# First chunk in halves of 64 times too, from one table of powers; the own key as a product of its own

## The chip, the cores and the metric

The kernel runs on one core of a Trainium2 chip. A core has a matrix engine (PE, whose weight loads are listed as PEld), a vector engine (DVE), a scalar engine (ACT), a general engine (POOL) and a queue engine (SP) that issues the transfers here. They run side by side; each works through its own list of instructions in order, and semaphores make one wait for another. [...] The metric is the device time of one execution in microseconds (us); lower is better.

## The reference, cut to what matters

An RWKV-style recurrence is followed by an MLP with gelu, all in fp32. Batch 4, 8 heads, 768 times, head size 48; the MLP has 384 inputs, 2048 hidden units and 384 outputs.

```python
for t in range(S):
    kt, vt, rt = (k[:, :, t], v[:, :, t], r[:, :, t])
    cur = np.einsum('bhd,bhe->bhde', u[None] * kt, vt)
    y[:, :, t] = np.einsum('bhd,bhde->bhe', rt, state + cur)
    state = w[None, :, :, None] * state + np.einsum('bhd,bhe->bhde', kt, vt)
...
x = y with the heads side by side            # 3072 tokens x 384
h = x @ w_in
g = 0.5 * h * (1.0 + erf(h / sqrt(2)))
return g @ w_out
```

`w` is a decay per head and channel. A key at time s counts at a later time t with the weight w^(t-1-s); the own key, at time t itself, counts with `u` in its place.

## The kernel before, in words

**Tiling.** Time is cut into six chunks of C = 128. A group is one pair of heads in one chunk, with all four batches, so there are 24 groups: `gi // 4` is the chunk, `PAIRS[gi % 4]` the pair. The 512 outputs (4 batches x 128 times) of the four groups of a chunk make one token tile of the MLP. The MLP of a tile is 16 steps over the hidden units, 96 steps in all. Each fp32 operand is split in a high and a low part (`wh`/`wl`, `xx`, `gh`/`gl`), and a step has 18 matmuls of 128x512: nine for the first layer into the bank `Hp` (`product1`, L602, three operand combinations times three parts of x) and nine for the second layer into the banks `O[0]` to `O[2]` (`product2`, L642). ACT reads `Hp` twice (L630 gives `gh`, L631 gives `gf`), and DVE makes `gl` of the two (L632). In the order of the program, PE does the nine first-layer matmuls of step m, then the nine second-layer matmuls of step m-1, in three operations of three, while ACT does the two gelu passes of step m. After 16 steps ACT and DVE copy the three `O` banks out (L676).

**The weights.** `w_split` takes each of the 16 weight pieces through passes on ACT (L330, L332, L340) and DVE (L334, L336, L338, L342), all within the first token tile.

**A group of chunks 1 to 5** (`prepare`, `products`, `state`, `past_scores`, `finish`) works in halves of 64 times. DVE multiplies r and k by powers of w from a table `E` (L479). POOL makes the key times its state power (L485) and the product r*k*u (L482, L488), DVE sums that over the channels (L491), and ACT spreads the sums on the diagonal of `Am` (L351). PE makes the scores of r with the scaled keys of the same half (L527), and DVE selects those of the past into `Am` (L576). PE adds up the output from the state before each half (L519, `old`) and from `Am` and v (L546, `new`), and makes the gain of the state in each half (L536, `gains`). DVE carries the state over a half (L569). `keep` splits the output into its high part on ACT (L367) and its low part on DVE (L368). The outputs lie in the PSUM tile `YU`, scores and gains in `AA`.

**A group of chunk 0** (`first_group`) works on all 128 times at once, with a table `W` of powers from -64 to 64: inverses by reciprocal (L271), scaling of r and k on DVE and POOL (L393), r*k (L399) and its sum with u on PE (L404), the diagonal on ACT, DVE or POOL (L351, L356), scores (L419), selects (L425), outputs (L439), state gains (L445). State powers are made on DVE (L281 to L285), turned by PE (L290) and copied (L293). The table `E` for the later chunks is cut out of `W` by eight transfers on SP's queue (L303).

**What sets the order.** `Plan` is a list scheduler written into the kernel: each step names its engine, a cost, a due time, and what it reads and writes by name (`"H"`, `"O0"`, `"Y"`). `Plan.run` emits the steps in the order of its own clock, with a lag (`LAG`) between engines, and fills gaps of PE with matmuls on zeros into `Hp` (L249, `heat`). The waits themselves are not made from these names. The Tile framework makes them from the tiles that each instruction reads and writes, in the order in which the steps are emitted.

**PSUM tiles before.** Two tiles have two banks each, and four have one:

```python
AA = psp.tile([128, 2, 512], F32, name="A")
YU = psp.tile([128, 2, 512], F32, name="Y")
Y, U = (YU[:, i] for i in range(2))
Hp = psp.tile([128, 512], F32, name="Hp")
O = [psp.tile([128, 512], F32, name=f"O{i}") for i in range(3)]
```

In chunk 0 the bank `Y` holds outputs, and `U` holds turned powers and state gains; the profile names both by their tile, "Y".

Of the kernel before, what the change touches and what calls it, by code (L numbers as in the profile page):

```python
# [27 lines left out]
HALF = 64  # L28
LP = 112
# [4 lines left out]
NEAR = 4  # L34
KEYS = C + 2
# [4 lines left out]
LOADS = (1, 2, 3, "w0", "w1", "u", 4, 5, "w2")  # L40

SCALE = ("pd", "d", "dd", "p")
PRODUCT = ("p", "p", "d", "p")
BONUS = ("pa", "aa", "pd", "pa")


class Plan:
# [6 lines left out]
    def __init__(self):  # L54
        self.ops, self.writer, self.readers, self.reads, self.filler = [], {}, {}, [], None
# [28 lines left out]
    def run(self):  # L84
# [14 lines left out]
        for _ in self.ops:  # L99
# [9 lines left out]
            if e == "pe" and self.filler:  # L109
                fill, buf, ns, room = self.filler  # L110
                while not unread and max(free[e], clear) + room < start:
                    fill()
                    free[e] = max(free[e], clear) + ns
# [9 lines left out]
            if self.filler:  # L123
                unread += sum(self.filler[1] in self.reads[m] for m in users[n])
# [10 lines left out]
def rwkv_gelu_mlp(tc, rkT, rkv, wuT, uN, wmlp, r, k, vT, w, u, out):  # L135
    nc = tc.nc
    with ExitStack() as ctx:
# [17 lines left out]
        wu_sb = sb([LP, 3 * NP], F32, "wu_sb", cst)  # L155
        w_sb = wu_sb[:, 0:NP]
        u_pair = wu_sb[:, NP:].rearrange("l (p j) -> l p j", j=2)
# [8 lines left out]
        W = sb([LP, NP, KEYS + C], F32, "W", pro)  # L166
        WKs = W[:, :, KEYS:]
        E = sb([LP, 2, NP, 2, HALF], F32, "E")
        P128 = sb([LP, NP], F32, "P128")
        WN = sb([C, NP, 2, D], F32, "WN", pro)  # L170
        WN2 = sb([C, NP, 2, D], F32, "WN2")
        T = [sb([LP, 2, NB, C], F32, f"T{i}", pro) for i in range(NP)] + [sb([LP, 2, NB, C], F32, f"Tb{i}") for i in range(2)]
        Ts = [sb([LP, 2, NB, C], F32, f"Ts{i}", pro) for i in range(NP)]
        RK = [sb([LP, NB, C], F32, f"RK{i}", pro) for i in range(NP)]
        N = [sb([C, 2, NB, 2 * D], F32, f"N{i}", pro) for i in range(NP)] + [sb([C, 3, NB, 2 * D], F32, f"Nb{i}") for i in range(2)]
        Am = [sb([C, 2, NB, C], F32, f"Am{i}") for i in range(2)] + [sb([C, 2, NB, C], F32, f"Am{i}", pro) for i in (2, 3)]
        cs = [sb([C, NB * 2], F32, f"cs{i}") for i in range(4)]
# [28 lines left out]
        def load_group(gi, at):  # L206
            s = slot(gi)
            dma(LP * 4096, at, lambda: nc.sync.dma_start(T[s], rkT[gi]), w=[f"T{s}"])
            if gi < NP:
                dma(C * 3072, at + 1, lambda: nc.sync.dma_start(N[s], rkv[gi, :, 1:]), w=[f"Nk{s}", f"Nv{s}"])  # L210
            else:
# [9 lines left out]
        def select(dst, base, cm, op):  # L221
# [14 lines left out]
        add("dve", 300, -20, lambda: nc.vector.memset(zeros.bitcast(F32), 0.0), w=["zeros"])  # L236
# [14 lines left out]
        def warm_up():  # L251
            for n in range(HEATS):
                heat((A + O + [Y, U])[n % 7])
            plan.filler = lambda: heat(Hp), "H", HEAT_NS, HEAT_ROOM

        add("pe", 430 * HEATS, 10, warm_up, r=["zeros"], w=["H", "A0", "A1", "O0", "O1", "O2", "Y", "U"])


        def powers():
            nc.vector.memset(W[:, :, HALF:HALF + 1], 1.0)  # L260
            nc.vector.tensor_scalar(out=W[:, :, HALF + 1:HALF + 2], in0=w_sb.unsqueeze(2), scalar1=WMIN, scalar2=WMAX,
                                    op0=ALU.max, op1=ALU.min)
            n = 1
            while n < HALF:
                pn = W[:, :, HALF + n:HALF + n + 1].to_broadcast([LP, NP, n])
                nc.vector.tensor_tensor(out=W[:, :, HALF + n + 1:HALF + 2 * n + 1],
                                        in0=W[:, :, HALF + 1:HALF + n + 1], in1=pn, op=ALU.mult)
                n *= 2

        def inverse(p0, p1):  # L270
            nc.vector.reciprocal(out=W[:, p0:p1, 0:HALF], in_=W[:, p0:p1, C:HALF:-1])  # L271

        add("dve", 1500, 5, powers, r=["w_sb"], w=["P"])
        first = PAIRS[0]
        add("dve", 480, 6, lambda: inverse(first, first + 1), r=["P"], w=[f"W{first}"])
        for p in PAIRS[1:]:
            add("dve", 480, LATER, lambda p=p: inverse(p, p + 1), r=["P"], w=[f"W{p}"])


        def state_powers():  # L280
            nc.vector.tensor_copy(out=WKs[:, :, 0:32], in_=W[:, :, 96:C])  # L281
            nc.vector.tensor_tensor(out=P128.unsqueeze(2), in0=W[:, :, C:C + 1], in1=W[:, :, C:C + 1], op=ALU.mult)
            nc.vector.tensor_tensor(out=WKs[:, :, 32:96], in0=W[:, :, HALF:C],
                                    in1=W[:, :, C:C + 1].to_broadcast([LP, NP, HALF]), op=ALU.mult)
            nc.vector.tensor_tensor(out=WKs[:, :, 96:C], in0=W[:, :, HALF:96],  # L285
# [609 lines left out]
```

## Time and profile before

| what | value |
|---|---|
| three timed runs | 513.5, 515.7 and 517.62 us; median 515.7 |
| the profiled execution | 512.43 us, of which the span from first to last instruction is 510.7 |
| busy PE, DVE, ACT, POOL | 488.2, 248.8, 213.6 and 88.6 us |
| mean granted clock of PE | 0.973 of full speed |
| first matmul of the MLP | 37.59 us after the span's start |
| gelu of the last step of the first token tile | at 126.94 us |

How to read the lines of the profile: a timeline row gives start, length, engine, line of the kernel, operation, output<-inputs by the names of the tiles, shapes and a count; where an engine had been idle, the end of the row names in brackets how long, and whose work released it. Consecutive matmuls of one line are put together in one row; their ends are modelled, so that rows of a running PE overlap, and the distance between the starts of rows is the pace. A window row gives, for a stretch, the busy time of each engine with its instructions, then the granted clock, the share of the transfers and their rate.

### The profile page before, as it was taken

The page shows a single profiled execution, that of the slowest core. Times are in us where ns is not written, and L with a number is a line of the kernel's source. Part 1 is how long each engine was busy: PE and PEld are TensorE (multiplying, and loading weights), DVE is VectorE, ACT ScalarE, POOL GpSimd, SP SyncE. Part 2 cuts the span into 40 slices and gives each one's busy share as a digit, 9 for nine tenths or more (in the row PEclk, how much of TensorE's full clock was granted, in tenths as well). Part 3 has the DMA queues.
Part 4 walks back from the last instruction along what each step waited for, and adds up shares of the span by engine and source line. Part 5 has one row for each costly group of instructions (what it writes and reads, how often), then busy time and mean ns, then how long its engine had stood idle before and what let it go on. Part 6 is the DMA issues. An engine that isn't in the chain of part 4 may idle for free.

```text
span 510.7 us, 10489 instructions
## 1 busy us (share of the span) xinstructions
PE 488.2 (96%) x4524; PEld 387.8 (76%) x4524; DVE 248.8 (49%) x363; ACT 213.6 (42%) x472; POOL 88.6 (17%) x80
## 2 busy tenths in 40 slices
PE   5998898999999999999999999999999999999995
PEld 4876676766778778787777778778778787888884
DVE  8959999998536424614425435424424311211111
ACT  2458758774444243333343443343442322322221
POOL 5850311213022022202022022022022000000000
PEclk8659999999999999999999999999999999999998
DMA  8864574822402303403302403303403000100001
GB/s 226 254 251 145 189 231 149 252 83 63 145 7 89 94 4 92 145 1 94 95 1 94 142 5 94 94 1 94 134 13 94 13 0 12 62 1 0 1 0 67
DMA packets 15107, 45.04 MB, mean 88 GB/s; under 512 B 3728, under 2 KB 4112, under 8 KB 15056
## 3 DMA queue, kind: packets, MB, share of 16 engines
q1 hardware_dynamic: 15056, 44.32, 27.8%
q8 instruction: 37, 0.61, 0.5%
q14 instruction: 14, 0.11, 0.1%
HBM read 37.16 MB, written 4.72 MB: 82 GB/s over the span
## 4 chain that ended last, share of the span: by engine, by line
PE 84%; DVE 11%; issue 2%; ACT 1%; DMA 1%; SPq 0%; DVEq 0%
PE Hp L602 37%; PE O L642 35%; PE Y L546 2%; PE Y L519 2%; PE A L527 2%; DVE wa L338 1%; DVE wl L342 1%; DVE Ts L393 1%; PE A L536 1%; PE Y L642 1%; DVE gl L632 1%; DVE wa L336 1%; DMA T<-in_rkT_dram 1%; DVE wa L334 1%; ACT wh L340 1%
## 5 line engine op out<-in xcount | busy, mean ns | idle before, releaser
L602 PE MATMUL Hp<-xx,wh 128*128 128x512 f32 x576 | 168.8, 400 | 0.8 <-ACT gf L631 0.5
L632 DVE TENSOR_TENSOR gl<-gf,gh 128x512 fp32r<-128x512 f32 x95 | 73.2, 770 | 193.9 <-ACT gf L631 193.8
L630 ACT ACTIVATE gh<-Hp 128x512 fp32r<-128x512 f32 x95 | 56.7, 597 | 183.6 <-PE Hp L602 183.5
L602 PEld LDWEIGHTS Hp<-xx,wh 128*128 128x128 f32 x576 | 105.8, 188 | 26.6 <-ACT gf L631 1.5
L642 PE MATMUL O<-gh,wh 128*128 128x512 f32 (+1 forms) x285 | 82.0, 395 | 6.2 <-ACT gh L630 6.2
L602 PE MATMUL Hp<-xx,wl 128*128 128x512 f32 x288 | 84.1, 399 | 0.7 <-DVE wl L342 0.3
L642 PE MATMUL O<-gh,wl 128*128 128x512 f32 (+1 forms) x285 | 80.8, 391 | 0.0
L642 PE MATMUL O<-gl,wh 128*128 128x512 f32 (+1 forms) x285 | 80.6, 390 | 0.0
L482 POOL TENSOR_TENSOR Nb<-Nb 128x384 f32<-128x384 f32 x20 | 22.6, 1131 | 294.9 <-DMA Nb<-in_rkv_dram 257.5
L642 PEld LDWEIGHTS O<-gh,wh 128*128 128x128 f32 x285 | 52.6, 188 | 23.4 <-ACT gh L630 11.9
L602 PEld LDWEIGHTS Hp<-xx,wl 128*128 128x128 f32 x288 | 53.5, 188 | 15.6 <-DVE wl L342 3.3
L642 PEld LDWEIGHTS O<-gl,wh 128*128 128x128 f32 x285 | 52.6, 188 | 11.9 <-DVE gl L632 0.2
L642 PEld LDWEIGHTS O<-gh,wl 128*128 128x128 f32 x285 | 52.6, 188 | 11.7
L351 ACT ACTIVATE Am<-diag,cs 128x64 f32<-128x64 f32 (+1 forms) x176 | 47.4, 345 | 22.8 <-DVE cs L491 22.7
L631 ACT ACTIVATE gf<-Hp 128x512 f32<-128x512 f32 x96 | 56.9, 593 | 0.0
L367 ACT CAST xx<-Y 112x512 fp32r<-112x512 f32 (+1 forms) x16 | 9.4, 587 | 41.7 <-PE Y L546 41.0
L479 DVE TENSOR_TENSOR Tb<-Tb,E 112x1024 f32<-112x1024 f32 x20 | 24.4, 1220 | 2.9 <-DMA Tb<-in_rkT_dram 2.9
L488 POOL TENSOR_TENSOR Nb<-Nb,u_sb 128x384 f32<-128x384 f32 x20 | 25.6, 1282 | 0.2
L569 DVE SCALAR_TENSOR_TENSOR Sb<-Sa,E,A 48x192 f32<-48x192 f32 x40 | 16.5, 413 | 16.0 <-PE A L536 15.4
L485 POOL TENSOR_TENSOR Nb<-Nb,WN 128x384 f32<-128x384 f32 x20 | 22.7, 1135 | 2.7 <-ACT WN L293 1.3
L576 DVE COPY_PREDICATED Am<-past,A 128x512 f32<-128x512 uint32 x20 | 14.8, 738 | 7.0 <-PE A L536 6.8
L342 DVE TENSOR_TENSOR wl<-wa,wh 128x768 fp32r<-128x768 f32 x16 | 16.7, 1042 | 1.9 <-ACT wh L340 1.7
(114 smaller groups left out, 396.1 us busy)
## 6 DMA issues: line engine op xcount, KB each, us to landing
raw<-in_wmlp_dram SPq DMA_DIRECT2D x16, 768.0 KB, 6.9
Nb<-in_rkv_dram SPq DMA_DIRECT2D x20, 576.0 KB, 5.4
Tb<-in_rkT_dram SPq DMA_DIRECT2D x20, 448.0 KB, 3.9
out_dram<-raw SPq DMA_DIRECT2D x5, 768.0 KB, 4.6
xx<-x SPq DMA_DIRECT2D x30, 64.0 KB, 3.9
T<-in_rkT_dram SPq DMA_DIRECT2D x4, 448.0 KB, 6.9
N<-in_rkv_dram SPq DMA_DIRECT2D x4, 384.0 KB, 9.5
out_dram<-raw SPq DMA_DIRECT2D x2, 256.0 KB, 2.8
```

The source lines that it names most:

```text
L342: add("dve", sdve(n), LATER, lambda: nc.vector.tensor_tensor(out=both(wl), in0=af, in1=both(wh).bitcast(F32), op=ALU.subtract), r=[A_, f"w ...
L351: add("act", sact(n) + 90, LATER, lambda b=b: nc.scalar.activation(out=am[:, j, b, :], in_=diag, func=AF.Copy, scale=sums[:, 2 * b + j:2 * ...
L479: add("dve", sdve(1024), LATER, lambda: nc.vector.tensor_tensor(out=flat, in0=flat, in1=E[:, 0, p].rearrange("l h i -> l (h i)").unsqueeze ...
L482: add("pool", pool(DM), LATER, lambda: nc.gpsimd.tensor_tensor(out=n[:, 0], in0=n[:, 0], in1=n[:, 1], op=ALU.mult), r=[NK], w=[NR])
L485: add("pool", pool(DM), LATER, lambda: nc.gpsimd.tensor_tensor(out=kn, in0=kn, in1=WN2[:, p].rearrange("s j d -> s (j d)").unsqueeze(1).to ...
L488: add("pool", pool(DM), LATER, lambda: nc.gpsimd.tensor_tensor(out=n[:, 0], in0=n[:, 0], in1=u_sb[:, p, :].unsqueeze(1).to_broadcast([C, N ...
L569: add("dve", 420, at, lambda l=l, x=x: nc.vector.scalar_tensor_tensor(out=out[quarter(1 - x)], in0=src[l], scalar=E[l, 1, p, h, 32:33], in ...
L602: nc.tensor.matmul(Hp, lhsT=wt[j][:, 0, k_ * 128:(k_ + 1) * 128], rhs=x[:, a, k_, :], start=start and k_ == ks[0], stop=stop and k_ == ks[-1])
L630: add("act", 480, LATER, lambda: nc.scalar.activation(out=high, in_=Hp, func=AF.Gelu), r=["H"], w=[GH])
L631: add("act", 480, LATER, lambda: nc.scalar.activation(out=gf, in_=Hp, func=AF.Gelu), r=["H"], w=["gf"])
L632: add("dve", dve(512), LATER, lambda: nc.vector.tensor_tensor(out=low, in0=gf, in1=high.bitcast(F32), op=ALU.subtract), r=["gf", GH], w=[GL])
L642: nc.tensor.matmul(dst[:, a:b], lhsT=wt[j][:, 1, d * 128:(d + 1) * 128], rhs=gt[:, a:b], start=(j == 0 and n == 0), stop=(j == NJ - 1 and ...
```

## The change

Chunk 0 goes through the same functions as the later chunks: halves of 64 times, the same `prepare`, `scores`, `gains`, `old`, `new`, `state` and `keep`, now methods on a `Group`. There is one table of powers: `E`, from -32 to 31, is built in place on DVE, and the eight transfers and the table `W` are gone. State powers are turned once.

In chunks 0 and 1 (`direct`) the own key's weight is a product of its own: ACT scales the scaled keys by u*w (`kb`), PE multiplies them with r (`own`, a second pass of `scores` into other columns of the score banks), and a DVE select on the diagonal puts them into `Am`, before the select of the past. POOL's r*k*u, DVE's sum and ACT's eight spreads go away there. `Am` is cleared once by POOL.

The gains move from the score banks to the output banks (columns 256 and up), and within `products` they come after `new`. Groups of chunk 0 alternate between two sets of four banks; the second set is made of the MLP's banks, and for that `O0` to `O2` and `Hp` become slices of one tile. Weight pieces with tiles of their own from the start go from four to eight, the order of the first loads changes, and the filler matmuls are held back while an odd group of chunk 0 uses the `Hp` bank.

```diff
-NEAR = 4
+NEAR = 8
-LOADS = (1, 2, 3, "w0", "w1", "u", 4, 5, "w2")
+LOADS = (1, "w0", 2, 3, "w1", 4, 5, "w2", "u")
+DIRECT = 2 * NP
...
         AA = psp.tile([128, 2, 512], F32, name="A")
+        YU = psp.tile([128, 2, 512], F32, name="Y")
+        OO = psp.tile([128, 4, 512], F32, name="O")
         A = [AA[:, i] for i in range(2)]
-        YU = psp.tile([128, 2, 512], F32, name="Y")
-        Y, U = (YU[:, i] for i in range(2))
-        Hp = psp.tile([128, 512], F32, name="Hp")
-        O = [psp.tile([128, 512], F32, name=f"O{i}") for i in range(3)]
+        O = [OO[:, i] for i in range(3)]
+        Hp = OO[:, 3]
+        SETS = (((AA, ["A0", "A1"]), (YU, ["Y0", "Y1"])), ((OO[:, 0:2], ["O0", "O1"]), (OO[:, 2:4], ["O2", "H"])))
...
+            if g.direct:
+                for h in range(2):
+                    add("act", sact(256) + 90, LATER, lambda h=h: nc.scalar.activation(
+                        out=g.kb[:, :, times(h)], in_=g.t[:, 1, :, times(h)], func=AF.Copy,
+                        scale=uw[:, 2 * g.p + h:2 * g.p + h + 1]), r=[g.T, "uw"], w=[f"{g.KB}{h}"])
+                return
...
+        def own(g):
+            scores(g, g.kb, U0)
...
+        def first_group(gi):
+            g = Group(gi)
+            prepare(g)
+            add("pe", 600, LATER, lambda: scores(g), r=[g.T], w=g.X)
+            add("pe", 600, LATER, lambda: own(g), r=[g.T, f"{g.KB}0", f"{g.KB}1"], w=g.X)
...
+            add("pe", 500, LATER, first_gains, r=[g.K, g.V], w=g.Y)
+            state(g, 0, LATER)
+            select(g, diag2, "diag", U0)
+            select(g, past2, "past", 0)
...
             def go():
-                if prev is not None:
-                    old()
-                if gi is not None:
-                    scores()
-                    gains()
-                if prev is not None:
-                    new()
+                if g:
+                    old(g)
+                if f:
+                    scores(f)
+                    if f.direct:
+                        own(f)
+                if g:
+                    new(g)
+                if f:
+                    gains(f)
```

More of the change, by code (lines that the diff above doesn't have):

```diff
@@ L54, in __init__ @@
     def __init__(self):
[L55 removed]
+        self.ops, self.writer, self.readers, self.reads, self.filler, self.hold = [], {}, {}, [], None, False
     def add(self, eng, ns, at, fn, r=(), w=()):
@@ L110, in run @@
                 fill, buf, ns, room = self.filler
-                while not unread and max(free[e], clear) + room < start:
+                while not unread and not self.hold and max(free[e], clear) + room < start:
                     fill()
@@ L123, in run @@
             if self.filler:
-                unread += sum(self.filler[1] in self.reads[m] for m in users[n])
+                unread += sum(self.filler[1] in self.reads[m] for m in users[n] if self.ops[n][0] == "pe")
                 if self.filler[1] in self.reads[n]:
@@ L268, in powers @@
                 n *= 2
[L270 to L277, printed above, removed]
-        def state_powers():
[L281 to L285, printed above, removed]
-                                    in1=P128.unsqueeze(2).to_broadcast([LP, NP, 32]), op=ALU.mult)
@@ L314, in rwkv_gelu_mlp @@
+        add("act", 500, LATER, lambda: nc.scalar.copy(
+            out=WN, in_=OO[:, 1].rearrange("s (p j x) -> s p j x", p=NP, x=64)[:, :, :, :D]), r=["O1"], w=["WN"])
         wbits = wmlp.bitcast(I32)
@@ new lines, in scores @@
+        def scores(g, keys=None, col=0):
+            for b in range(NB):
+                for h in range(2):
+                    for x in range(2):
+                        k_ = (g.t[:, 1] if keys is None else keys)[quarter(x), b, times(h)]
+                        nc.tensor.matmul(g.x[times(h), x, col + b * HALF:col + (b + 1) * HALF], lhsT=k_,
+                                         rhs=g.t[quarter(x), 0, b, times(h)], start=True, stop=True)
+        def own(g):
+            scores(g, g.kb, U0)
@@ new lines, in gains, with old @@
+        def gains(g):
+            for b in range(NB):
+                for x in range(2):
+                    for h in range(2 if g.more else 1):
+                        nc.tensor.matmul(g.y[quarter(x), h, U0 + b * D:U0 + (b + 1) * D], lhsT=g.kn[times(h), b, heads(x)],
+                                         rhs=g.vn[times(h), b, heads(x)], start=True, stop=True)
+        def old(g):
+            for b in range(NB):
+                for j in range(2):
+                    for h in range(1 if g.c == 0 else 0, 2):
+                        l = quarter(j ^ h)
+                        nc.tensor.matmul(g.y[quarter(j), h, b * HALF:(b + 1) * HALF], lhsT=g.s[h][l, b, :],
+                                         rhs=g.t[l, 0, b, times(h)], start=(b == 0 and not spreads(g)), stop=False,
+                                         skip_group_check=True)
@@ new lines, in new @@
+        def new(g):
+            nc.tensor.drain()
+            for b in range(NB):
+                for j in range(2):
+                    for h in range(2):
+                        nc.tensor.matmul(g.y[quarter(j), h, b * HALF:(b + 1) * HALF], lhsT=g.vn[times(h), b, heads(j ^ h)],
+                                         rhs=g.am[times(h), j ^ h, b, :], stop=True, skip_group_check=True,
+                                         start=(g.c == 0 and h == 0 and b == 0 and not spreads(g)))
+        spreads = lambda g: g.c == 0 and g.p < 3
@@ new lines, in group @@
+        def group(gi, at):
+            f = Group(gi) if gi < NG else None
+            g = Group(gi - 1) if gi > NP else None
+            if f:
+                prepare(f)
+            products(g, f)
+            if f:
+                state(f, 0, LATER)
+                if f.direct:
+                    select(f, diag2, "diag", U0)
+                select(f, past2, "past", 0)
+            if g:
+                keep(g, at)
+            if f and f.more:
+                state(f, 1, at + 20000)
```

432 lines of the change are left out of this document (159 added, 273 removed).

## The prediction, made before the result was known

> **What bounds the kernel now.** I read the page first: the busy time of each engine and, of the chain of waits that ended last, its shares by engine and by line.
>
> ```profile
> PE 488.2 (96%) x4524; PEld 387.8 (76%) x4524; DVE 248.8 (49%) x363; ACT 213.6 (42%) x472; POOL 88.6 (17%) x80
> PE 84%; DVE 11%; issue 2%; ACT 1%; DMA 1%; SPq 0%; DVEq 0%
> ```
>
> PE carries the end. An average over stages hides where the other engines rule, so I then asked for the windows before the first MLP matmul, through the first token tile, and after it.
>
> ```profile
> 0.00:37.60 37.60, 31.11 (x235) 25.41 (x235) 28.43 (x43) 16.11 (x41) 24.37 (x26) 0.68 0.81 248
> 37.60:127.00 89.40, 81.25 (x874) 58.89 (x871) 85.52 (x115) 64.29 (x121) 18.35 (x12) 1.00 0.49 159
> 127.00:490.00 363.00, 360.96 (x3348) 291.14 (x3347) 131.66 (x202) 128.99 (x303) 45.83 (x42) 1.00 0.19 57
> ```
>
> The first number pair is the stretch, then PE, PEld, DVE, ACT and POOL. In the second stretch DVE is busy 85.52 of 89.40 us and PE waits for it; in the third PE is busy 360.96 of 363. Last I read the timelines, for the pace of a step.
>
> ```profile
> 139.91 0.86 PE L602 MATMUL Hp<-xx,wh 128*128 128x512 f32 x3
> 140.61 0.86 PE L642 MATMUL O<-gh,wh 128*128 128x512 f32 x3
> 141.31 0.86 PE L642 MATMUL O<-gh,wl 128*128 128x512 f32 x3
> 142.01 0.86 PE L642 MATMUL O<-gl,wh 128*128 128x512 f32 x3
> 140.81 0.60 ACT L630 ACTIVATE gh<-Hp 128x512 fp32r<-128x512 f32 x1 [3.11 <-PE Hp L602]
> 141.31 0.59 ACT L631 ACTIVATE gf<-Hp 128x512 f32<-128x512 f32 x1
> 149.22 0.60 ACT L630 ACTIVATE gh<-Hp 128x512 fp32r<-128x512 f32 x1 [1.22 <-PE Hp L602]
> 155.84 0.60 ACT L630 ACTIVATE gh<-Hp 128x512 fp32r<-128x512 f32 x1 [1.69 <-PE Hp L602]
> ```
>
> Three matmuls start every 0.70 us. Two steps lie between the gelus at 140.81 and 149.22, so a step is 8.41 / 2 = 4.205 us; a step with a group in it is 155.84 - 149.22 = 6.62, so a group costs PE 2.42. Both gelu passes run while PE writes the `O` banks: three second-layer operations hide them. That cover is what the change takes away.
>
> **A wait that the change adds.** Before, `Hp`, `O0`, `O1` and `O2` are tiles of their own; after, they are slices of one tile. What that does can be seen on the one tile whose banks the old program already uses apart, "Y": its first bank holds outputs (written by L439, read by L367 and L368), its second state gains (written by L445, read by L450).
>
> ```profile
> 29.44 1.95 PE L439 MATMUL Y<-Am,N 128*48 128x128 f32 x16
> 31.81 0.40 ACT L351 ACTIVATE Am<-diag,cs 128x128 f32<-128x128 f32 x1
> 31.96 0.88 PE L445 MATMUL Y<-N 128*48 128x48 f32 x16 [0.58 <-ACT WN L293]
> 32.89 0.58 ACT L367 CAST xx<-Y 128x512 fp32r<-128x512 f32 x1 [0.68 <-PE Y L445]
> 35.36 0.69 DVE L368 TENSOR_TENSOR xx<-Y,xx 128x512 fp32r<-128x512 f32 x1 [2.38 <-PE Y L445]
> 36.08 0.64 ACT L450 COPY Sa<-Y 48x192 f32<-48x192 f32 x2 [0.40 <-DVE xx L368]
> ```
>
> L367 reads the first bank, which L439 had finished at 29.44 + 1.95 = 31.39; ACT was free at 32.21. It sat until 32.84, when L445 had finished writing the other bank. L450 reads the second bank and waited until 36.05 for DVE's read of the first. So the framework orders any two engines on one tile, whichever bank each touches, reads against reads included. In the changed program, then, ACT's gelu of `Hp` waits for the last second-layer matmul emitted before it, and the next matmul into any `O` bank waits for the gelu. Queued behind that matmul are all later ones of PE, and behind the gelu the `gl` on DVE.
>
> [...]
>
> **The price of one such wait** stands where PE already waits for a gelu:
>
> ```profile
> 108.60 0.86 PE L602 MATMUL Hp<-xx,wh 128*128 128x512 f32 x3
> 109.50 0.60 ACT L630 ACTIVATE gh<-Hp 128x512 fp32r<-128x512 f32 x1 [0.57 <-PE Hp L602]
> 109.99 0.59 ACT L631 ACTIVATE gf<-Hp 128x512 f32<-128x512 f32 x1
> 110.15 0.96 PE L642 MATMUL O<-gh,wh 128*128 128x512 f32 x3 [0.69 <-ACT gh L630]
> 110.94 0.87 PE L642 MATMUL O<-gh,wl 128*128 128x512 f32 x3
> ```
>
> The next operation would have started at 108.60 + 0.70 = 109.30 and started at 110.15: 0.85 lost. The operation after it came 0.79 later in place of 0.70: 0.1 more. One wait costs 0.95.
>
> How many per step? The scheduler's costs decide: gelu `gh` is placed 220 ns after the first layer ends and takes 480, so `gf` is placed at 700 ns; the second-layer operations are placed at 0, 648 and 1296. The order is operation, `gh`, operation, `gf`, operation: two waits, 1.90 us. Where ACT and PE stand a little differently, both passes are emitted together and PE waits once for both, which ends 0.49 later (109.50 to 109.99): 0.95 + 0.49 = 1.44. The margin between the two is only 52 ns, so I take seven steps in ten as two waits: 0.7 x 1.90 + 0.3 x 1.44 = 1.76 us. Ends: 1.44 and 1.90. For 94 steps (96 less a first and a last): **+166 us**, between 135 and 179.
>
> The copies of `O` now stop PE as well, three reads a tile:
>
> ```profile
> 131.90 1.07 ACT L676 COPY raw<-O 128x512 f32<-128x512 f32 x2
> ```
>
> A copy is half of 1.07, close to a gelu; between none and three waits of 0.95 for each of five tiles is 0 to 14. I take **+8**.
>
> **The start.** Until 37.59 the changed part rules.
>
> ```profile
> 1.28 4.55 DMA T<-in_rkT_dram
> 13.33 9.14 SPq L303 DMA_DIRECT2D E<-W  x8
> L393 DVE TENSOR_TENSOR Ts<-T,W 112x1024 f32<-112x1024 f32 x1 | 1.2, 1214 | 0.0
> L425 DVE COPY_PREDICATED Am<-past,O 128x512 f32<-128x512 uint32 x4 | 2.8, 726 | 4.1 <-PE O L419 3.4 <-ACT Am L351 0.8
> L283 DVE TENSOR_TENSOR W<-W 112x256 f32<-112x256 f32 x1 | 0.4, 414 | 0.0
> 36.43 0.95 DVE L342 TENSOR_TENSOR wl<-wa,wh 128x768 fp32r<-128x768 f32 x1
> 42.48 0.86 DVE L569 SCALAR_TENSOR_TENSOR Sb<-Sa,E,A 48x192 f32<-48x192 f32 x2
> 37.59 0.50 PE L602 MATMUL Hp<-xx,wh 128*128 128x512 f32 x1
> ```
>
> Removed: the eight transfers that held SP's queue for 9.14 us, with the loads of chunk 1 behind them; the inverses and long powers, the r*k sums and one turn of powers. DVE's work from the landing of the first T (1.28 + 4.55 = 5.83) to the first MLP matmul is afterwards four scalings of 1.21, eight selects of 0.73, four low parts of 0.69 (L368 above), two state powers of 0.41, two groups' state steps of 0.86, and one weight piece in four passes of at most 0.95: 4.8 + 5.8 + 2.8 + 0.8 + 1.7 + 3.8 = 19.7 us. So the MLP can't start before 25.5. The other end is 37.6, no gain: odd groups and the filler matmuls now share one tile, so their selects, gains and fills go one after the other. I take 31, near the middle: **-6.6**, between -12 and 0.
>
> **The first tile.** From 37.59 to the sixteenth gelu,
>
> ```profile
> 126.94 0.60 ACT L630 ACTIVATE gh<-Hp 128x512 fp32r<-128x512 f32 x1 [0.81 <-PE Hp L602]
> 40.57 0.69 PE L527 MATMUL A<-Tb 48*64 48x64 f32 x32
> 41.09 0.54 PE L536 MATMUL A<-Nb 64*48 64x48 f32 x32
> ```
>
> 89.35 us pass. At the steady pace it would be 15.5 steps (65.2), the first group (40.57 to 41.63, 1.1) and four whole groups (9.7), in all 76.0; 13.4 are lost to DVE. With the new waits PE needs about 103 us for this tile, DVE's 85.5 fit beside it, and nearly all of the 13.4 is no longer late, since PE is later: I leave 2, so **-11.4** (between -13.4 and -6).
>
> The added products of chunk 1 are 32 matmuls for each of four groups, 0.52 each by 40.57 to 41.09: **+2**. In chunk 1, POOL loses two passes, ACT eight spreads for two scalings, and DVE changes a sum for a select of 0.73. None is on the path of a tile that PE rules; if that cover were gone, the selects would add at most 4 x 0.73 = 2.9. Gains after the new products are the same matmuls in another order: 0; a late select behind them costs at most their 0.54 a group, 11 over 20 groups, and nothing while PE has a step's products to do. Eight weight tiles in place of four take away a gate that no quoted wait shows: 0.
>
> **Sum**, against the profiled 512.4: - 6.6 - 11.4 + 2 + 166 + 8 = 670. The median of the runs, 515.7, lies 0.6% above that execution, so the forecast is **673 us**. Ends: 512 - 12 - 13 + 135 = 622, and 512 - 6 + 2 + 179 + 14 + 3 + 3 = 707.
>
> **The rivals.**
>
> *Banks stay apart, so it gets faster.* [...] For it: ACT and PE run side by side in steady state now. Against it: the three waits on "Y". Then only the start counts. With the same DVE work in the first tile and the MLP starting at 28, between 25.5 and 31, the time is 515.7 - 9.6 = 506; it is faster as soon as the start gains more than the 2 us of added products. Chance 0.11, of which 0.09 is over 1% faster.
>
> *One wait per step.* If nearly every step emits both passes together, the stalls are 135 and the copies few: 515.7 - 6.6 - 11.4 + 2 + 135 + 4 = 639. The 52 ns margin speaks for some of it. Chance 0.2.
>
> *The own products become the bound.* If PE in chunk 1 waited for ACT's scaled keys in each group, that is two ACT passes of about 0.6 (a gelu's length) and 0.95 for the wait, 2.2 us for four groups, 9 us: 515.7 + 9 - 9.6 = 515 without the shared tile. Against it: ACT is busy 64.29 of 89.40 us in the first tile, so it has room. It is the part of the first rival that ends within 1%, 0.02.
>
> **How the numbers follow.** Two waits in most steps: 0.68; one wait: 0.2; banks apart: 0.11; something else: 0.01. The first is the likeliest, so 673. The range 615 to 707 holds both slow cases with their unknown terms, 622 to 707 and 639, a little widened below for a better start; it leaves out the faster rival and a tenth of the slow cases, 2 in 10. Over 1% slower 0.89, within 1% 0.02, over 1% faster 0.09; 1% is about what the three runs (513.5 to 517.62) can tell from no change.
>
> **What would show it.** In the changed profile, PE's idle time before L642's counterpart should name ACT's gelu, in steady state too, with about 0.7 us per row and 130 to 190 such waits; the distance between gelus should be 5.6 to 6.1 us, against 4.2; PE's busy share should fall below 85%. The first MLP matmul should come at 26 to 37 us. If the gelus still come every 4.2 us and run beside the `O` matmuls, the step that failed is the reading of "Y" as a rule for every tile of several banks.

## The result, and the profile after

The changed kernel takes 687.8 us (median; 685.1 to 690.7) where the kernel before, run beside it, takes 516.3: a ratio of 1.333, 95% interval 1.325 to 1.342. The profiled execution took 686.5 us, its span is 684.7. The forecast was 673, in a range of 615 to 707.

The page of the changed kernel, busy time and then the chain of waits by engine and by line:

```profile
PE 527.2 (77%) x5006; PEld 379.1 (55%) x5006; DVE 249.0 (36%) x366; ACT 214.7 (31%) x435; POOL 75.6 (11%) x66
PE 75%; ACT 16%; issue 4%; DVE 2%; DMA 1%; SPq 0%; ACTq 0%; DVEq 0%
```

PE fell from 96% to 77% of the span, and ACT's share of the chain rose from 1% to 16%, while ACT's busy time hardly grew (213.6 to 214.7). A bank is here a slice of 512 fp32 columns on 128 partitions of a PSUM tile; in this profile PE writes the `O` banks and ACT and DVE read them. The view of waits names who is waited for (engine, line <- releaser: us of idle time in all, times, longest). In the changed file L543 is `product1`, L583 `product2`, L571 and L572 are the two gelu passes, L614 and L617 the copies of `O`:

```profile
PE O L583 <- ACT gf L572: 76.9, 94, 1.2
PE O L583 <- ACT gh L571: 46.7, 68, 0.7
PE O L543 <- DVE raw L614: 2.8, 2, 1.4
PE O L543 <- ACT raw L617: 2.5, 3, 1.2
```

There are 162 waits for a gelu: every one of 94 steps waits for the second pass, and 68 of them for the first as well. The timeline of two steps in steady state shows how:

```profile
194.50 0.86 PE L583 MATMUL O<-gh,wh 128*128 128x512 f32 x3
195.39 0.60 ACT L571 ACTIVATE gh<-O 128x512 fp32r<-128x512 f32 x1 [3.85 <-PE O L583]
196.04 0.97 PE L583 MATMUL O<-gh,wl 128*128 128x512 f32 x3 [0.69 <-ACT gh L571]
197.04 0.60 ACT L572 ACTIVATE gf<-O 128x512 f32<-128x512 f32 x1 [1.06 <-PE O L583]
197.69 0.97 PE L583 MATMUL O<-gl,wh 128*128 128x512 f32 x3 [0.69 <-ACT gf L572]
201.50 0.60 ACT L571 ACTIVATE gh<-O 128x512 fp32r<-128x512 f32 x1 [1.81 <-PE O L583]
```

Every operation on the tile "O" waits for the one before it on the other engine: matmuls into the `O` banks, a gelu pass out of the `Hp` bank, matmuls, a pass, matmuls. The gelus stand 201.50 - 195.39 = 6.11 us apart; before it was 4.205.

The start went the other way than forecast. PE's timeline up to the first MLP matmul, rows that end an idle time:

```profile
16.52 0.45 PE L408 MATMUL Y<-T,Sb 48*48 48x64 f32 x3 [2.83 <-issue]
24.30 0.48 PE L389 MATMUL O<-T 48*64 48x64 f32 x4 [3.60 <-issue]
32.58 0.92 PE L400 MATMUL O<-N 64*48 64x48 f32 x32 [2.94 <-issue]
42.87 0.76 PE L543 MATMUL O<-xx,wh 128*128 128x512 f32 x1 [2.64 <-DVE Sa L441]
```

The first MLP matmul comes at 42.87 us (before: 37.59). Two rows, at 16.52 and 24.30, stand in the middle of a run of equal matmuls and name no releaser ("issue"). The row at 32.58 names none either, but it starts 0.10 after DVE's last select out of the shared tile (31.77 + 0.71 = 32.48), so I read it as a wait for that select. The first gelu follows at 47.08 (before: 43.34), the sixteenth at 147.94 (before: 126.94).

So the 174.0 us of longer span are 5.3 up to the first MLP matmul, 15.7 from there to the sixteenth gelu (105.07 for 89.35), and 153.0 after it.

### The profile page after: what moved, and what is told of

Same layout as the page of the kernel before. It is cut to its first block, busy times and chain, and to the rows that moved or that the text cites. A ratio compares the mean times of both kernels' runs of the same rounds, so it can differ in the third digit from the quotient of the medians.

```text
span 684.7 us, 11450 instructions
## 1 busy us (share of the span) xinstructions
PE 527.2 (77%) x5006; PEld 379.1 (55%) x5006; DVE 249.0 (36%) x366; ACT 214.7 (31%) x435; POOL 75.6 (11%) x66
## 4 chain that ended last, share of the span: by engine, by line
PE 75%; ACT 16%; issue 4%; DVE 2%; DMA 1%; SPq 0%; ACTq 0%; DVEq 0%
PE O L583 35%; PE O L543 30%; ACT gf L572 8%; ACT gh L571 8%; PE Y L418 2%; PE A L389 2%; PE Y L408 2%; PE Y L400 1%; DMA T<-in_rkT_dram 1%; PE O L389 1%; PE Y L583 1%; ACT raw L617 1%; DVE wa L321 0%; DVE wl L325 0%; PE O L428 0%
## 5 line engine op out<-in xcount | busy, mean ns | idle before, releaser
L543 PE MATMUL O<-xx,wh 128*128 128x512 f32 x576 | 169.8, 402 | 5.9 <-DVE Sa L441 2.6
L571 ACT ACTIVATE gh<-O 128x512 fp32r<-128x512 f32 x95 | 56.7, 597 | 269.7 <-PE O L583 265.0
L583 PE MATMUL O<-gh,wl 128*128 128x512 f32 (+1 forms) x285 | 88.7, 418 | 60.7 <-ACT gh L571 43.2
L583 PE MATMUL O<-gl,wh 128*128 128x512 f32 (+1 forms) x285 | 87.5, 414 | 47.7 <-ACT gf L572 44.1
L543 PEld LDWEIGHTS O<-xx,wh 128*128 128x128 f32 x576 | 106.4, 190 | 31.4 <-ACT wa L313 2.8
L583 PEld LDWEIGHTS O<-gh,wl 128*128 128x128 f32 x285 | 47.3, 188 | 97.7 <-ACT gh L571 70.6
L583 PE MATMUL O<-gh,wh 128*128 128x512 f32 (+1 forms) x285 | 82.0, 395 | 16.1 <-ACT gf L572 15.4
L583 PEld LDWEIGHTS O<-gl,wh 128*128 128x128 f32 x285 | 47.4, 188 | 82.7 <-ACT gf L572 71.5
L543 PE MATMUL O<-xx,wl 128*128 128x512 f32 x288 | 84.7, 401 | 3.8 <-DVE raw L614 1.4
L572 ACT ACTIVATE gf<-O 128x512 f32<-128x512 f32 x96 | 57.2, 596 | 73.3 <-PE O L583 73.3
L583 PEld LDWEIGHTS O<-gh,wh 128*128 128x128 f32 x285 | 52.4, 188 | 34.0 <-ACT gf L572 21.3
L543 PEld LDWEIGHTS O<-xx,wl 128*128 128x128 f32 x288 | 54.0, 190 | 18.3 <-DVE raw L614 1.8
L380 ACT ACTIVATE Am<-diag,cs 128x64 f32<-128x64 f32 x128 | 33.8, 337 | 16.8 <-DVE cs L375 16.8
L356 DVE TENSOR_TENSOR Tb<-Tb,E 112x1024 f32<-112x1024 f32 x20 | 32.5, 1627 | 0.9 <-DMA Tb<-in_rkT_dram 0.9
L441 DVE SCALAR_TENSOR_TENSOR Sb<-Sa,E,Y 48x192 f32<-48x192 f32 x40 | 16.5, 413 | 33.9 <-ACT xx L460 28.4
L325 DVE TENSOR_TENSOR wl<-wa,wh 128x768 fp32r<-128x768 f32 x16 | 16.5, 1032 | 4.0 <-ACT wh L323 3.8
```

What stands on the lines that cost most here:

```text
L325: add("dve", sdve(n), LATER, lambda: nc.vector.tensor_tensor(out=both(wl), in0=af, in1=both(wh).bitcast(F32), op=ALU.subtract), r=[A_, f"w ...
L356: add("dve", sdve(1024), LATER, lambda: nc.vector.tensor_tensor(out=flat, in0=flat, in1=E[:, 0, g.p].rearrange("l h i -> l (h i)").unsquee ...
L380: add("act", sact(HALF) + 60, LATER, lambda x=x, b=b: nc.scalar.activation(out=g.am[:, x, b, :], in_=diag2, func=AF.Copy, scale=g.sums[:, ...
L543: nc.tensor.matmul(Hp, lhsT=wt[j][:, 0, k_ * 128:(k_ + 1) * 128], rhs=x[:, a, k_, :], start=start and k_ == ks[0], stop=stop and k_ == ks[-1])
L571: add("act", 480, LATER, lambda: nc.scalar.activation(out=high, in_=Hp, func=AF.Gelu), r=["H"], w=[GH])
L572: add("act", 480, LATER, lambda: nc.scalar.activation(out=gf, in_=Hp, func=AF.Gelu), r=["H"], w=["gf"])
```

## The experiments

Each kernel was timed beside the kernel before on the same chip. The kernel before took 512.6 us beside the merge alone, own tiles, the first try and the held-back loads; 514.1 beside the two passes as one step, only `O` shared, own tiles after chunk 0 and own products in chunk 0; 513.2 beside two early tiles and beside the two combinations; 513.1 beside low parts on POOL. Across these, ratios are compared.

**Merge alone.** The kernel before, with only the four banks made one tile:

```diff
-        Hp = psp.tile([128, 512], F32, name="Hp")
-        O = [psp.tile([128, 512], F32, name=f"O{i}") for i in range(3)]
+        OO = psp.tile([128, 4, 512], F32, name="O")
+        O = [OO[:, i] for i in range(3)]
+        Hp = OO[:, 3]
```

> The kernel before, with one edit: `Hp` and the three `O` banks become slices of one tile. Nothing of the start, the first chunk or the own products changes. Theory (the shared tile orders PE and ACT): as emitted, about 67 steps wait twice and 28 once, 67 x 1.90 + 28 x 1.44 = 168 us of stalls, + 8 for the copies, - 11 for the first tile's wait for DVE that is then no longer late: about 681 us, and a gelu every 6.1 us. Rival (the time came from the rewritten first chunk or the own products): within 1% of 516, a gelu every 4.2 us.

Measured: 682.3 us, ratio 1.333 (1.328 to 1.338). The waits of this run, with this file's L643 for `product2` and L631 and L632 for the gelus:

```profile
PE O L643 <- ACT gf L632: 76.5, 89, 3.3
PE O L643 <- ACT gh L631: 46.0, 67, 0.7
PE O L603 <- ACT gf L632: 3.7, 5, 0.7
```

This is the same 1.333 as the whole change, with the same waits. Three lines that compute nothing make a loss as large as the whole one; what is left of the change adds up to about nothing beside it. By itself it is not nothing, as the next runs show.

**Own tiles.** The changed kernel, with the banks apart again:

```diff
-        OO = psp.tile([128, 4, 512], F32, name="O")
+        OO = psp.tile([128, 2, 512], F32, name="O")
...
-        O = [OO[:, i] for i in range(3)]
-        Hp = OO[:, 3]
-        SETS = (((AA, ["A0", "A1"]), (YU, ["Y0", "Y1"])), ((OO[:, 0:2], ["O0", "O1"]), (OO[:, 2:4], ["O2", "H"])))
+        O = [OO[:, 0], OO[:, 1], psp.tile([128, 512], F32, name="O2")]
+        Hp = psp.tile([128, 512], F32, name="Hp")
+        SETS = (((AA, ["A0", "A1"]), (YU, ["Y0", "Y1"])), ((OO[:, 0:2], ["O0", "O1"]), (YU, ["Y0", "Y1"])))
```

> The changed kernel with the banks as tiles of their own again: one tile of two banks for O0 and O1, one each for O2 and Hp. Odd groups of chunk 0 keep O0 and O1 for their scores, but their outputs go to the same two banks as those of even groups. Theory: of 687.8 the stalls (167) and the copies (8 to 9) go, and of the start the 5.6 us that PE waited on the shared tile; the first token tile loses up to 11.4 to DVE again: 507 to 518, a gelu every 4.2 us, the first MLP matmul at about 37, with the two PE gaps of 2.8 and 3.6 us that name no releaser still there. Rival (the rewrite of the first chunk costs time by itself): over 530. Rival (it is worth what the prediction's faster case said): 506.

Measured: 519.4 us, ratio 1.015 (1.011 to 1.019), first MLP matmul at 36.27, first gelu at 45.98. Its timeline in steady state:

```profile
140.16 0.86 PE L583 MATMUL O<-gh,wh 128*128 128x512 f32 x3
140.36 0.60 ACT L571 ACTIVATE gh<-Hp 128x512 fp32r<-128x512 f32 x1 [0.98 <-PE Hp L543]
140.85 0.59 ACT L572 ACTIVATE gf<-Hp 128x512 f32<-128x512 f32 x1
140.85 0.86 PE L583 MATMUL O<-gh,wl 128*128 128x512 f32 x3
144.56 0.60 ACT L571 ACTIVATE gh<-Hp 128x512 fp32r<-128x512 f32 x1 [3.11 <-PE Hp L543]
```

PE writes `O` while ACT reads `Hp`, and a step is 144.56 - 140.36 = 4.20 us again. The 168 us are gone, so the loss belongs to the tile and not to the rewritten first chunk. But the kernel isn't faster than the one before, it is 1.5% slower: the rival of 506 fell too.

**Only `O` shared.** As before, but O0 to O2 one tile of three banks, with `Hp` alone:

```diff
-        OO = psp.tile([128, 2, 512], F32, name="O")
+        OO = psp.tile([128, 3, 512], F32, name="O")
...
-        O = [OO[:, 0], OO[:, 1], psp.tile([128, 512], F32, name="O2")]
+        O = [OO[:, i] for i in range(3)]
```

> The kernel with own tiles, but O0 to O2 slices of one tile of three banks; only `Hp` is a tile of its own. Theory (only `Hp` in the tile makes the gelus wait; the copies of `O` are the small rest): a gelu every 4.2 us, and of the 8.6 us that the copies cost in the changed kernel some part comes back: 519 to 528. Rival (slices of one tile cost a step time whether or not the gelu's bank is among them): over 600.

Measured: 521.4 us, ratio 1.011 (1.007 to 1.015): no different from own tiles that these runs could tell. With only `Hp` apart a gelu comes every 4.20 us (142.00 to 146.20): slices of one tile cost these steps nothing, as only one engine at a time had business in it. Where two had, in the copies, they still waited: ACT's copies waited 3.0 us in four waits for DVE's (0.76 at 138.57), read after read, which with own tiles they didn't. `Hp` in the tile makes the loss, and most of what the copies cost too: in the changed kernel five of their seven waits stop `product1`, which writes `Hp`.

**Both passes together, a first try.** One cost of the planner, in the changed kernel:

```diff
-            add("act", 480, LATER, lambda: nc.scalar.activation(out=high, in_=Hp, func=AF.Gelu), r=["H"], w=[GH])
+            add("act", 400, LATER, lambda: nc.scalar.activation(out=high, in_=Hp, func=AF.Gelu), r=["H"], w=[GH])
             add("act", 480, LATER, lambda: nc.scalar.activation(out=gf, in_=Hp, func=AF.Gelu), r=["H"], w=["gf"])
```

> The changed kernel with one planner cost edited: each gelu pass is planned at 400 in place of 480, so that the second is placed before the next second-layer operation and both passes are mostly emitted together: 17 steps with two waits and 79 with one, against 69 and 27. Theory: 52 steps save 1.90 - 1.44 = 0.46 us each, 24 us, so about 664, and a steady step of 5.65 us in place of 6.11. Rival (a step loses the whole round from PE to ACT and back however the passes are emitted): 688.

Measured: 690.5 us, ratio 1.348 (1.343 to 1.353). The expectation speaks of each pass; the edit changed the cost of the first alone. The timeline shows why the 24 us did not come:

```profile
258.09 0.86 PE L583 MATMUL O<-gh,wh 128*128 128x512 f32 x3
259.05 0.60 ACT L572 ACTIVATE gf<-O 128x512 f32<-128x512 f32 x1 [1.63 <-PE O L583]
259.70 0.96 PE L583 MATMUL O<-gh,wl 128*128 128x512 f32 x3 [0.75 <-ACT gf L572]
260.69 0.60 ACT L571 ACTIVATE gh<-O 128x512 fp32r<-128x512 f32 x1 [0.81 <-PE O L583]
261.35 0.96 PE L583 MATMUL O<-gl,wh 128*128 128x512 f32 x3 [0.69 <-ACT gh L571]
```

With the new cost the planner turned the two passes round, `gf` first, and still put a matmul operation between them. A count that looks only for matmuls between `gh` and a later `gf` takes this order for one with a single wait; in the run PE waits for a gelu 169 times, against 162 in the changed kernel. The run doesn't test the price of a wait; it shows how easily a planner's cost does something else than meant.

**Both passes together, one step.** The changed kernel with the passes as one step of the planner:

```diff
-            add("act", 480, LATER, lambda: nc.scalar.activation(out=high, in_=Hp, func=AF.Gelu), r=["H"], w=[GH])
-            add("act", 480, LATER, lambda: nc.scalar.activation(out=gf, in_=Hp, func=AF.Gelu), r=["H"], w=["gf"])
+            add("act", 960, LATER, lambda: [nc.scalar.activation(out=o, in_=Hp, func=AF.Gelu) for o in (high, gf)],
+                r=["H"], w=[GH, "gf"])
```

> The changed kernel with the two gelu passes as one step of the planner, planned at 960, so that no matmul is ever put between them and their order stays. Theory (each separate meeting of PE and ACT on the shared tile costs 0.95, and a step with one meeting costs 1.44 against 1.90): 68 steps save 0.46 us, 31 us in all, so about 657, a steady step of 5.65 us, and half as many waits of PE for a gelu (about 95 in place of 162). Rival (a step loses the round from PE to ACT and back twice however the passes are placed): 688.

Measured: 656.7 us, ratio 1.275 (1.270 to 1.280). The waits of this run, whose two passes are both on L571:

```profile
PE O L583 <- ACT gf L571: 106.1, 92, 1.2
PE O L543 <- ACT gf L571: 3.5, 3, 1.2
```

and its timeline:

```profile
188.59 0.60 ACT L571 ACTIVATE gh<-O 128x512 fp32r<-128x512 f32 x1 [4.55 <-PE O L583]
189.09 0.59 ACT L571 ACTIVATE gf<-O 128x512 f32<-128x512 f32 x1
189.73 0.97 PE L583 MATMUL O<-gh,wl 128*128 128x512 f32 x3 [1.17 <-ACT gf L571]
194.23 0.60 ACT L571 ACTIVATE gh<-O 128x512 fp32r<-128x512 f32 x1 [2.50 <-PE O L583]
```

A step is 194.23 - 188.59 = 5.64 us, and 95 waits are left. The prices of 1.90 for a step with two waits and 1.44 for a step with one stand.

**Own tiles after chunk 0.** The changed kernel with its shared tile in chunk 0 alone:

```diff
-        OO = psp.tile([128, 4, 512], F32, name="O")
+        first = ctx.enter_context(ExitStack())
+        OO = first.enter_context(tc.tile_pool(name="psf", bufs=1, space=PSUM)).tile([128, 4, 512], F32, name="O")
...
+        def own_banks():
+            first.close()
+            pm = ctx.enter_context(tc.tile_pool(name="psm", bufs=1, space=PSUM, reuse_waits="tile"))
+            bank[0:3] = (pm.tile([128, 512], F32, name=f"O{i}") for i in range(3))
+            bank[3] = pm.tile([128, 512], F32, name="Hp")
+
+        add("do", 0, 0, own_banks, w=["O0", "O1", "O2", "H"])
```

> The changed kernel with its one tile of four banks in chunk 0 only: when the last group of chunk 0 is done with it, the tile is given back and O0, O1, O2 and Hp are taken anew as tiles of their own, before the first MLP matmul. Theory: the start is that of the changed kernel, first MLP matmul at 42 to 44 us, first gelu at 47, and from there a gelu every 4.2 us: the stalls of 167 and the copies of 8.6 go, and the 11.4 that the first token tile loses to DVE comes back or stays away, so 512 to 526, near 520. Rival (some of the 171 us is not the MLP's waits on the shared tile): over 540.

Measured: 520.2 us, ratio 1.011 (1.007 to 1.014), first MLP matmul at 42.00, first gelu at 46.03, and in steady state a gelu every 4.20 us (147.39 to 151.59). This is the start as the change has it, and the MLP as the kernel before has it. The loss of a third is the MLP's alone.

**Two early tiles.** The same, with two tiles of two banks in chunk 0:

```diff
-        OO = first.enter_context(tc.tile_pool(name="psf", bufs=1, space=PSUM)).tile([128, 4, 512], F32, name="O")
+        psf = first.enter_context(tc.tile_pool(name="psf", bufs=1, space=PSUM))
+        OO, QQ = (psf.tile([128, 2, 512], F32, name=x) for x in "OQ")
...
-        SETS = (((AA, ["A0", "A1"]), (YU, ["Y0", "Y1"])), ((OO[:, 0:2], ["O0", "O1"]), (OO[:, 2:4], ["O2", "H"])))
+        SETS = (((AA, ["A0", "A1"]), (YU, ["Y0", "Y1"])), ((OO[:, 0:2], ["O0", "O1"]), (QQ, ["O2", "H"])))
```

> The kernel that gives its four-bank tile back after chunk 0, with that tile split in two of two banks for chunk 0 as well: scores of odd groups in one, outputs and gains in the other. Theory (the shared tile also orders the start: waits of 2.9 and 2.6 us of PE on DVE there): the first MLP matmul at 36 to 38 in place of 42.0, and 3 to 5 us less in all, a ratio to the kernel before of 1.000 to 1.005 in place of 1.011. Rival (the first token tile is paced by DVE, so that an earlier start is spent in waiting): the same 1.011.

Measured: 518.3 us, ratio 1.011 (1.008 to 1.014), first MLP matmul at 43.46. The theory failed. The waits of 2.9 and 2.6 us are those of the changed kernel; in the kernel that gives its tile back, PE's largest waits for DVE after 30 us are only 1.44, 0.39 and 0.33, and with two tiles 0.81 and 0.33. Taking them away does not bring the MLP forward: PE's second gap without a releaser was 4.92 us here (4.10 there), and its wait for DVE's scaling of the second group 3.07 (1.69). A wait on one engine's row is no price while other work is as late.

**Loads held back.** The kernel with own tiles; four tiny transfers, each behind the one before, delay the later loads until the first group's output is there:

```diff
+            if gi == 0:
...
+                for i in range(4):
+                    dma(64, 6.5, lambda i=i: nc.sync.dma_start(
+                        gate_sb[i], gate_sb[i - 1] if i else x3[0:1, 0, 0:16].bitcast(F32)), r=["x3h"], w=gated)
+                loads(4, len(LOADS))
```

> The previous kernel but one with own tiles, and the loads of the second and third weight piece, of `u` and of the groups 4 and 5 held back behind four tiny chained transfers that begin when the first group's output is there, so that no large transfer runs from about 16 to 26 us. Theory (PE's two gaps without a releaser, 2.8 us at 13.7 and 3.6 us at 20.7 in the changed kernel, are its instructions arriving late behind saturated transfers): the second gap shrinks to under 1 us, the first stays or shrinks a little, the first MLP matmul comes 2 to 4 us earlier and the whole time falls by 1 to 4. Rival (the gaps come at fixed places in the instruction stream whatever the transfers do): both gaps stay, the time is the same or, with the later loads, up to 5 us longer.

Measured: 516.9 us, ratio 1.009 (1.006 to 1.012); 2.5 us less than own tiles on the same chip, which four runs of each (516.6 to 518.6 against 517.5 to 521.1) hardly tell apart. The windows of the kernel with own tiles (stretch, then PE, PEld, DVE, ACT, POOL, granted clock, share of the transfers, GB/s):

```profile
17.50:21.20 3.70, 3.62 (x127) 2.96 (x128) 2.57 (x5) 2.98 (x5) 0.00 (x0) 0.67 1.02 296
21.20:25.30 4.10, 0.01 (x2) 0.01 (x2) 3.42 (x5) 0.00 (x0) 0.46 (x1) 0.50 1.03 292
```

its PE row at the end of the gap:

```profile
25.29 0.48 PE L389 MATMUL O<-T,KB 48*64 48x64 f32 x6 [4.10 <-issue]
```

and its queue of instruction loads from 22.5 to 24 us (packets, MB, share of 16 engines):

```profile
q8 instruction: 1, 0.02, 5.3%
```

The same windows with the loads held back:

```profile
17.50:21.20 3.70, 2.69 (x99) 2.69 (x102) 1.52 (x3) 2.17 (x5) 0.73 (x1) 0.61 0.07 24
21.20:25.30 4.10, 3.34 (x81) 2.63 (x74) 3.61 (x5) 1.74 (x5) 0.00 (x0) 0.50 0.02 4
```

and the timeline there:

```profile
22.19 1.13 PE L389 MATMUL O<-T,KB 48*64 48x64 f32 x32
23.10 0.86 PE L400 MATMUL Y<-N 64*48 64x48 f32 x32
```

With the transfers at 1.03 of their engines PE stopped in the middle of 32 equal matmuls for 4.10 us, and went on after a packet of instructions had come. With the transfers at 0.02 to 0.07 the 32 run through, though a packet comes then too (between 22 and 24 us). So the loads made the second gap. That what PE lacked was its instructions, queued behind the loads, is what the packet and the stop amid equal matmuls point to; no run shows it directly. The first gap (2.16 us here, ended at 18.51, with the transfers at 0.87 from 15.0 to 17.5) stayed, as expected. The first MLP matmul came only 0.7 us earlier, at 35.57, and the first gelu no earlier, at 46.04, though 2 to 4 had been expected.

**Own products in chunk 0 only.** The kernel with own tiles, with one constant changed:

```diff
-DIRECT = 2 * NP
+DIRECT = NP
```

> The kernel with own tiles, with the own products in chunk 0 only; chunk 1 is prepared as before (POOL's r*k*u, DVE's sum, ACT's eight spreads). Theory (the prediction's term for the added products of chunk 1): 2 us less than with own tiles alone, 517 to 518. Rival (in the first token tile DVE sets the pace, and its sum of 0.55 is as long as a select of 0.73): within 0.5 us of it, 519. Rival (POOL's two passes of 1.1 and 1.6 us or the spreads come late): 520 to 526.

Measured: 513.7 us, ratio 0.999 (0.995 to 1.004), against 1.015 with them in chunk 1 too. All three numbers were off. By the ratios they cost 0.0157 x 513 = 8 us here (5 to 11 by the intervals), and (1.0088 - 1.0013) x 513 = 4 us between the two kernels with loads held back (1.5 to 6). In the profiled executions, one each, the sixteenth gelu comes 1.4 us earlier without them (130.46 to 129.02), and 5.0 with loads held back (131.82 to 126.80). The groups of the first token tile with own tiles (line, engine, operation x count | busy us, mean ns | idle before):

```profile
L389 PE MATMUL A<-Tb,KB 48*64 48x64 f32 x128 | 3.0, 241 | 0.0
L400 PE MATMUL Y<-Nb 64*48 64x48 f32 x160 | 3.3, 220 | 1.5 <-issue 1.5
```

The added products are 3.0 us, and one more gap without a releaser stands behind them, 1.5, which these rows do not have in the kernel with own products in chunk 0 only: together 4.5. What the rest is, if there is any, no run tells.

**Both, and with two early tiles.** Two combinations of the edits above: loads held back and own products in chunk 0 only, on the kernel with own tiles, and on the kernel with two early tiles.

> The kernel with own tiles, with the later loads held back and the own products in chunk 0 only; odd groups' outputs are in the banks of the even groups. Theory (the two are independent): 2.5 us less than with the own products in chunk 0 only, a ratio to the kernel before of 0.994 to 0.996. Rival (gating hides behind DVE's pace in the first token tile): 0.999.

> The kernel with two early tiles, with the later loads held back and with the own products in chunk 0 only. Theory (gated loads are worth 2 to 3 us, the own products of chunk 1 about 5): a ratio to the kernel before of 0.985 to 0.995, 507 to 512. Rival (the first token tile is paced by DVE): 0.995 to 1.005.

Measured: 513.7 us, ratio 1.001 (0.998 to 1.005), and 515.1, ratio 1.001 (0.998 to 1.005). The numbers of the rivals hold: neither holding back the loads nor two tiles gains anything more that these runs can tell.

**Low parts on POOL.** The former of the two, with half of one pass moved off DVE in the first token tile:

```diff
-            add("dve", sdve(n), LATER, lambda: nc.vector.tensor_tensor(
+            eng, on = ("pool", nc.gpsimd) if j % 2 else ("dve", nc.vector)
+            add(eng, pool(n) if eng == "pool" else sdve(n), LATER, lambda: on.tensor_tensor(
                 out=both(wl), in0=af, in1=both(wh).bitcast(F32), op=ALU.subtract),
```

> The last kernel (gated loads, own products in chunk 0 only), with the subtraction that makes the low part of a weight piece on POOL in place of DVE for every second piece, eight of sixteen. Theory (DVE sets the pace of the first token tile, busy 87.69 of 94.00 us from 36 to 130, while POOL is busy 27.81): DVE gives up 8 x 1.03 = 8.2 us, of which the tile gains 4 to 8: a ratio to the kernel before of 0.985 to 0.993, 506 to 510, the sixteenth gelu at 119 to 123 in place of 126.8. Rival (the pace there is PE's own, the wait for DVE only fills its slack): 1.001. Rival (POOL takes over 2 us for such a pass, and the pieces come late): 1.002 or more.

Measured: 513.3 us, ratio 1.000 (0.998 to 1.003), the sixteenth gelu at 128.15 for 126.80. DVE was busy 86.89 us from 36 to 130, for 87.69 without the edit. Groups of that stretch without the edit:

```profile
L321 DVE CUSTOM_DVE_ANT_0 wa<-wa,wb 128x1536 uint16<-128x1536 uint16 x15 | 16.4, 1096 | 0.2
L325 DVE TENSOR_TENSOR wl<-wa,wh 128x768 fp32r<-128x768 f32 x15 | 15.7, 1045 | 0.8 <-ACT wh L323 0.7
L317 DVE TENSOR_SCALAR wa<-wa 128x768 int32<-128x768 int32 x14 | 7.4, 549 | 0.0
```

and with it:

```profile
L326 POOL TENSOR_TENSOR wl<-wa,wh 128x768 fp32r<-128x768 f32 x8 | 18.5, 2311 | 27.7 <-ACT wh L323 27.7
L326 DVE TENSOR_TENSOR wl<-wa,wh 128x768 fp32r<-128x768 f32 x7 | 6.6, 947 | 0.9 <-ACT wh L323 0.9
L321 DVE CUSTOM_DVE_ANT_0 wa<-wa,wb 128x1536 uint16<-128x1536 uint16 x15 | 17.4, 1161 | 0.2
L317 DVE TENSOR_SCALAR wa<-wa 128x768 int32<-128x768 int32 x14 | 13.0, 937 | 0.0
```

Eight subtractions left DVE (15.7 us became 6.6), but with POOL busy 43.89 us of the stretch in place of 27.81, two of the passes that stayed grew longer: L317 from 549 to 937 ns, 5.6 us in all, and L321 from 1096 to 1161. What made them longer no run here shows. Whether DVE paces that tile stays open, since the edit did not take its load away. The chain of waits through these 94 us without the edit is 42.4 us DVE, 31.6 PE and 10.2 loads of weights, so DVE is not alone in it.

No version beats the kernel before by more than can be measured.

## Why the prediction was right, point by point

*The reading of "Y" as a rule for every tile of several banks* held: the merge alone costs what the whole change costs, own tiles give it back. With own tiles PE writes `O` while ACT reads `Hp`, at 4.20 us a step; with one tile they take turns, at 6.11: the waits are drawn by the program, per tile.

*The price of a wait and the count*: 94 steps, 68 with two waits and 26 with one, are 68 x 1.90 + 26 x 1.44 = 166.6 us, against 166. The share of seven steps in ten was a guess from a margin of 52 ns; that 68 of 94 is 0.72 is luck in part. A step with two waits was to be 4.205 + 1.90 = 6.105 and is 6.11. After the sixteenth gelu 65 steps with two waits and 15 with one make 145.1, with the copies 153.7; the span grew by 153.0 there. That last pair is the check by time; the 166.6 only has the prices with the counts put right. One number from one stall of the old trace (0.95) carried the forecast.

*The copies*: +8 against seven waits with 6.8 us of idle time and 0.26 more behind each (0.95 less the 0.69 that a row shows), 8.6.

*The first tile*: 14 waits for `gf` and 3 for `gh` there are 3 x 1.90 + 11 x 1.44 = 21.5. Of the 105.07 us, 76.0 of steady work, 2 of own products and these leave 5.6 lost, where I left 2: 7.8 of the 13.4 disappeared, not 11.4. The step's direction was right. Part of the 5.6 may be own products, which cost more than the 2.

*The start* is the step that failed: -6.6 was forecast, +5.3 measured, outside the ends of -12 and 0. I priced it by DVE's work alone. That sum was not far off: from 5.83 to 42.87 us DVE is busy 20.02, for the 19.7 I added up, though not with the same passes alone. What failed is to take it for what sets the start. The windows of the changed kernel's start, and two of the kernel before:

```profile
0.00:18.00 18.00, 12.34 (x260) 10.04 (x264) 11.79 (x25) 6.72 (x17) 6.29 (x14) 0.86 0.89 293
18.00:30.00 12.00, 7.95 (x220) 7.05 (x212) 3.73 (x7) 4.27 (x8) 1.99 (x2) 0.50 0.66 204
30.00:37.60 7.60, 4.93 (x88) 4.29 (x88) 5.25 (x8) 2.81 (x8) 0.00 (x0) 0.50 0.34 106
```

```profile
18.00:30.00 12.00, 11.94 (x80) 10.09 (x80) 8.33 (x13) 6.20 (x16) 8.28 (x7) 0.56 0.83 209
30.00:37.60 7.60, 7.02 (x83) 5.24 (x79) 4.46 (x6) 4.74 (x10) 4.61 (x5) 0.58 0.57 234
```

From 18 to 30 DVE works 3.73 of 12.00 us: it is not the bound. Nor is PE by its work, 7.95 of 12.00, where the kernel before has 11.94. PE runs 260 + 220 + 88 = 568 matmuls up to 37.6, where the kernel before ran 242 in the same stretches, at a granted clock of 0.50 from 18 on (before: 0.56 and 0.58), and stops in the gaps shown above and for other engines. And "no gain" was no bound: nothing in the profile excluded a loss. Which of these sets the first gelu is not settled: without the shared tile, without the second gap, and with two early tiles it still came at 45.98, 46.04 and 47.32, against 43.34 before. The mark was badly chosen as well: with own tiles the first MLP matmul comes earlier than before (36.27) and the first gelu later.

Nor does the first gelu set the time. With two early tiles, loads held back and own products in chunk 0 only it comes at 41.15, earlier than before, and the sixteenth still at 129.93 (before: 126.94); with own tiles and own products in chunk 0 only the first comes at 49.38, the latest of the kernels whose MLP has its own tiles, and the sixteenth at 129.02. From the sixteenth gelu to the end these two take 384.2 and 384.3 us, and the kernel before 383.8. In the first of them, what the earlier start gained was spent again in the first token tile.

*The own products*: +2 was forecast; 4 to 8 is what the ratios give. *The sum*: of 16.5 us between 670 and 686.5, the start is 11.9, the first tile 3.6, the stalls and the copies 0.6 each.

*The rivals.* "One wait per step" is the kernel with both passes as one step: 639 was given, and with the 15.5 us of start and first tile that I had wrong it would be 654.5; it took 656.7. "Banks apart" would not have been 506 but about what own tiles take, 519: the start gains nothing there, and the own products cost more.

*The marks.* PE's idle time names the gelus with 0.7 to 0.8 us per wait (46.7 / 68 and 76.9 / 94), 162 times; a step without a group is 5.52 to 6.18, mostly 6.11; PE is at 77%. The mark for the first MLP matmul, 26 to 37, is the one that was missed.

## What to carry to other kernels

Where waits are drawn from tiles, as here, two banks in one PSUM tile were not used by two engines at once (6.11 us a step for 4.20 with own tiles): a tile must hold only what one engine at a time has business with, and banks lent to another stage are better given back and taken anew (520 us against 688 for the same start). One existing stall, priced from its rows as start of next minus due start, and a count of how often the new order repeats it, gave the growth after the first token tile within 1% (153.7 for 153.0). A lower bound by one engine's work is no estimate of a start: here no engine was busy all through it (from 18 to 30 us PE 7.95 of 12.00 and DVE 3.73), and taking away one wait after another did not bring the time down.

## What the runs showed that was not expected

PE seems to run out of instructions; no run shows that directly. With 568 matmuls in the first 37.6 us in place of 242, PE stopped for 2.83 and 3.60 us in the middle of runs of equal matmuls, in the kernel with own tiles for 4.10, and went on after a packet on the queue of instruction loads; with the large transfers held back the gap of 4.10 us was gone. In the changed kernel, too, one packet of that queue falls in each of the two gaps (between 14 and 15 us, and between 21.5 and 22). Up to 36 us there are four of them; the kernel before has one, between 20 and 22 us, and PE runs on beside it, without idle time from 11.35 to 31. The changed kernel's page has this queue's total:

```profile
q8 instruction: 41, 0.67, 0.4%
```

That is 16 KB a packet (0.67 MB in 41), and a packet for every 244 of the 2 x 5006 matmuls and weight loads of PE; in the kernel before it is 37 packets for 2 x 4524, one for every 245. The packets grow with PE's work by these two counts; whose instructions they carry the page does not say.
